# New load order, a TensorE spin and new hand-written orders at both ends of a fused attention and adapter kernel

## The chip, the cores and the metric

The kernel runs on one core of one Trainium2 chip. The metric is the device time of one execution in microseconds (us); three runs of the kernel before gave a median of 393.7 us (393.56 to 393.74). Profiles are of one execution each, and all times inside a profile count from the start of its span.

The engines are named as the profile names them. PE is TensorE's matmul and PEld its weight load, DVE is VectorE, ACT is ScalarE, POOL is GpSimd, SP is SyncE (it only issues DMAs here). "SPq", "ACTq" and "POOLq" are the queues that issue DMAs.

## The reference

Attention over a spatially reduced key grid, and a mixture of eight small adapters on its result. Four batches, 12288 queries of 128 channels each; keys and values are the 4x4 means of a 384x32 grid (768 positions), multiplied by one 128x128 matrix.

```
kv_pool = kv.reshape(B, H//4, 4, W//4, 4, C).mean(axis=(2, 4))
k = v = kv_pool.reshape(B, -1, C) @ w_sr
x = softmax(q @ k.T / sqrt(C)) @ v
logits = x @ w_gate                  # 8 experts, the top two are taken
out = x + sum over the two: weight_e * ((x @ A[e]) @ B[e])
```

## The kernel before, in words

**Tiling.** The 49152 queries are cut into 96 chunks of 512 (24 per batch); four chunks make a group of 2048 queries, loaded together. The 768 keys are six blocks of 128, and are made in three parts h = 0, 1, 2 of two blocks each.

**The stages of a chunk k**, by the names that the order lists use:
- `sc k r` (line 244): scores against the two key blocks of part r. Two 128x512 matmuls into the PSUM tile `sg` (two buffers of two banks), then ACT's exponential into `em`.
- `at k s` (line 254): six matmuls that add the weighted values of 128 queries into the PSUM tile `acc` (one buffer of two banks). The last of its 137 columns carries the sum of weights. `pt k lo hi` (line 423) does the same for key blocks lo to hi of all four quarters.
- `nm k` (line 262): DVE takes the reciprocal and multiplies, which gives `xn`, with the 8 gate logits beside the 128 channels.
- `tp k` (line 281): DVE's eight largest; `ro k` (line 290) and `ga k` (line 308): the weights of the two experts, on POOL with a tanh on ACT.
- `tt x h` (line 317): PE transposes `xn` of chunk x and `hg` of chunk h into one PSUM tile, DVE (V) or ACT (A) copies it out. `dn k` (line 341): down projection into PSUM; `ge k` (line 346): DVE multiplies by the weights, giving `hg`; `up k` (line 355): up projection; `fi k` (line 360): DVE adds `xn` and SP stores 256 KB. The tiles of `tt`, `dn` and `up` share the PSUM tag `mb` with two buffers of one bank.
- Pieces for the ends: `xt`/`cx` (lines 388 and 398) and `hb`/`ht`/`ch` (lines 405 to 413) are the two halves of `tt` apart, `dn2`, `ge2`, `up2` the stages by halves, `af` (line 455) an add and a store, `ca` and `pd` (lines 462 and 467) the same add as a copy on ACT and an add on POOL.

**Order.** Every instruction is recorded in program order on its engine (`tc.keep_in_program_order`, line 65), so the order within an engine is that of the code. Chunks 14 to 71 follow a fixed pattern per chunk (`slot`, line 551). Chunks 0 to 13 and 72 to 95 follow two strings of items written out by hand (lines 579 and 601).

**The first keys.** Batch 0's grid is loaded in fp32 by 24 DMAs of 256 KB (line 98): per part h, four rows r and two halves x. DVE adds row pairs (`ad h i`, line 173), PE transposes with fp32 identity matmuls that also sum the remaining eight pieces (`ky`, line 187), DVE scales (line 206), PE projects (`k2`, line 209; `va`, line 215) and DVE copies out. Later batches are summed on POOL (`pa`, line 162) from 512 KB loads (`kv`, line 96).

**The queries.** Groups 0 and 1 are loaded in fp32 (line 105) and transposed by PE (`tq`, line 107). All later groups are cast to bf16 into DRAM by a DMA that POOL issues (`cq`, line 77, 1 MB read and 512 KB written) and transposed by a DMA that SP issues (`lq`, line 82). The first two casts are issued by `first_casts` (line 506): POOL copies one element of a tile that is being loaded, and so waits for it, then issues both. Before, the element is one of the last load of group 1 (`cs1`).

Of the kernel before, what the change touches and what calls it, by code (L numbers as in the profile page):

```python
# [20 lines left out]
def kernel(  # L21
# [10 lines left out]
    nc = tc.nc  # L32
# [74 lines left out]
    def turn_q(g, m, engine):  # L107
        if g not in qT:
            qT[g] = qpool.tile([P, GT], BF16, tag="qT", name="qT")
        ps = mtile([P, S, P], name="qT_ps")  # L110
        for i in range(S):
            mm(ps[:, i], q_f[g][:, m * S + i], id_f, is_transpose=True,
               start=(i == 0), stop=(i == S - 1))
        o = qT[g][:, m * T:(m + 1) * T].rearrange("p (s t) -> p s t", s=S)
        if engine is nc.scalar:
            keep(nc.scalar.copy(o, ps))
        else:
            keep(nc.vector.tensor_copy(o, ps))
# [6 lines left out]
    load_q(0, 0, GC * S)  # L125
    for h in range(3):
        for r in range(4):
            for x in range(2):
                load_kv(0, h, r, x)
    for m in range(GC):  # L130
        load_q(1, m * S, m * S + S)
    b_f = const.tile([P, C], FP32)
    keep(nc.sync.dma_start(b_f, moe_B.rearrange("e r c -> (e r) c")))
    a_f = const.tile([P, P], FP32)
    keep(nc.sync.dma_start(a_f, moe_A.rearrange("e c r -> c e r")))


    warm = const.tile([P, 1], FP32)
    nc.vector.memset(warm, 0.0)
    keep(nc.scalar.activation(warm, warm, AF.Exp, bias=0.0, scale=1.0))  # L140
    id_f = const.tile([P, P], FP32)
    make_identity(nc, id_f)
    id_bf = const.tile([P, P], BF16)
    nc.vector.tensor_copy(id_bf, id_f)
    wext = const.tile([P, VC], FP32)
    nc.vector.tensor_copy(wext[:, 0:C], w_sr_sb)
    wT_ps = mtile([P, C], name="wT_ps")
    mm(wT_ps, w_sr_sb, id_f, is_transpose=True, start=True, stop=True)
    wT = const.tile([P, C], FP32)
    nc.vector.tensor_copy(wT, wT_ps)  # L150
    w2_ps = mtile([P, E], name="w2_ps")
    mm(w2_ps, wT, w_gate_sb, start=True, stop=True)
    nc.vector.tensor_copy(wext[:, C:VC], w2_ps)


    kfT, vx = {}, {}

    def prepare(b, adder):
# [3 lines left out]
        def pool_step(h, step, lo, hi):  # L162
            t = kvr[b, h]
            if step < 3:
                u, v = t[:, 0].rearrange("p g c -> p (g c)"), t[:, step + 1].rearrange("p g c -> p (g c)")
            else:
                w = 2 * C if step == 3 else C
                u, v = t[:, 0, :, 0:w], t[:, 0, :, w:2 * w]
                keep(adder.tensor_tensor(u, u, v, op=ALU.add))
                return  # L170
            keep(adder.tensor_tensor(u[:, lo:hi], u[:, lo:hi], v[:, lo:hi], op=ALU.add))  # L171

        def pair_step(h, r, x):
            u, v = (kvr[b, h][:, r + i, x] for i in range(2))
            keep(adder.tensor_tensor(u, u, v, op=ALU.add))

        for h in range(3):
            if adder is nc.vector:
                sums.append([lambda h=h, r=r, x=x: pair_step(h, r, x)
                             for r in (0, 2) for x in range(2)])  # L180
                continue
# [5 lines left out]
        def keys(h, half=None):  # L187
            if h == 0 and half != 1:
                st["kpT"] = prep.tile([P, J, P], FP32, tag="kpT", name="kpT")
                kfT[b] = per_b.tile([P, J, P], BF16, tag="kfT", name="kfT")  # L190
            kpT = st["kpT"]
            if half != 1:
                st["ps"] = mtile([P, 2, P], name="kpT_ps")
            ps = st["ps"]
            if adder is nc.vector:
                parts = [(r, i, c) for r in (0, 2) for i in range(2) for c in range(4)]
            else:
                parts = [(0, i, 0) for i in range(2)]
            for n, (r, i, c) in enumerate(parts):
                if half is not None and r // 2 != half:  # L200
                    continue
                mm(ps[:, i], kvr[b, h][:, r, i, c * C:(c + 1) * C], id_f, is_transpose=True,
                   start=(n == 0), stop=(n == len(parts) - 1))
            if half == 0:
                return
            keep(nc.vector.tensor_scalar(kpT[:, 2 * h:2 * h + 2], ps, 1.0 / 16.0, None,
                                         op0=ALU.mult))

        def keys2(h):
            kpT = st["kpT"]  # L210
            ps = mtile([P, 2, P], name="kfT_ps")
            mm(ps, w_sr_sb, kpT[:, 2 * h:2 * h + 2], start=True, stop=True)
            keep(nc.vector.tensor_copy(kfT[b][:, 2 * h:2 * h + 2], ps))  # L213

        def values(h):
# [7 lines left out]
            if adder is not nc.vector:  # L223
                st["vb", h] = prep.tile([P, 2, C], BF16, tag="vb", name="vb")
                keep(nc.vector.tensor_copy(st["vb", h], ps[:, :, 0:C]))
# [8 lines left out]
        for h in range(3):  # L234
            for f in (keys, keys2, values) if adder is nc.vector else (keys, values, turn):
                rest.append(lambda h=h, f=f, **how: f(h, **how))
# [17 lines left out]
    def attend(k, s):  # L254
        b = k // NB
        if k not in acc:
            acc[k] = ps_a.tile([P, S, 256], FP32, tag="acc", name="acc")
        o = acc[k][:, s, 0:VE]
        for j in range(J):
            mm(o, em[k][:, j, s * P:(s + 1) * P], vx[b][:, j], start=(j == 0), stop=(j == J - 1))  # L260
# [11 lines left out]


# [16 lines left out]
    def route(k0):  # L290
        n = size[k0] * S
        eng = nc.gpsimd if k0 > 1 else nc.vector
# [74 lines left out]
    def bank(pool):  # L367
# [20 lines left out]
    def turn_x(k, pool):  # L388
        xT[k] = quad(bank(pool).bitcast(BF16), pool)
        xb = xn[k].bitcast(U16)[:, :, 1::2].bitcast(BF16)  # L390
        for s in range(S):
            mm(xT[k][:, s // 2, s % 2], xb[:, s, 0:C], id_bf, is_transpose=True,
               start=(s % 2 == 0), stop=(s % 2 == 1))

    def copy(engine, o, i):
        keep(nc.scalar.copy(o, i) if engine == "A" else nc.vector.tensor_copy(o, i))  # L396

    def fetch_x(k, engine):
        sb = run.tile([P, S, P], BF16, tag="tt1", name="tt1")
        copy(engine, four(sb), xT[k])  # L400
        xT[k] = sb
# [3 lines left out]
    def hold_h(k, pool):  # L405
        hps[k] = quad(bank(pool).bitcast(BF16), pool)

    def turn_h(k, lo=0, hi=S):
        for s in range(lo, hi):
            mm(hps[k][:, s // 2, s % 2], hg[k][:, s], id_bf, is_transpose=True,  # L410
               start=(s % 2 == 0), stop=(s % 2 == 1))

    def fetch_h(k, lo=0, hi=S, engine="A"):
        if lo == 0:
            hgT[k] = run.tile([P, S, P], BF16, tag="tt1", name="tt1")
        copy(engine, part(four(hgT[k]), lo, hi), part(hps[k], lo, hi))

    def hold_acc(k, pool="sg"):
        acc[k] = bank(pool)
# [3 lines left out]
    def attend_part(k, lo, hi):  # L423
        for s in range(S):
            for j in range(lo, hi):
                mm(acc[k][:, s, 0:VE], em[k][:, j, s * P:(s + 1) * P], vx[k // NB][:, j],
                   start=(j == 0 and s % 2 == 0), stop=(j == J - 1 and s % 2 == 1))

    def down_into(k, pool):
        hp[k] = quad(bank(pool), pool)  # L430
        for s in range(S):
            mm(hp[k][:, s // 2, s % 2], xT[k][:, s], a_bf, start=(s % 2 == 0), stop=(s % 2 == 1))

    def gate_part(k, lo, hi):
        if lo == 0:
# [3 lines left out]
        keep(nc.vector.tensor_tensor(  # L439
            part(four(hg[k]).rearrange("p a b (e r) -> p a (b e) r", e=E), lo, hi),  # L440
            part(four(hp[k]).rearrange("p a b (e r) -> p a (b e) r", e=E), lo, hi),
            part(g4, lo, hi).unsqueeze(3).broadcast_to([P, (hi - lo) // 2, 2 * E, RK]), op=ALU.mult))

    def hold_d(k, pool):
        dp[k] = quad(bank(pool), pool)

    def up_part(k, lo, hi):
        for s in range(lo, hi):
            mm(dp[k][:, s // 2, s % 2], hgT[k][:, s], b_bf, start=(s % 2 == 0), stop=(s % 2 == 1))
# [5 lines left out]
    def add_here(k, lo, hi, queue="SP"):  # L455
        osb = opool.tile([P, S, C], FP32, tag="osb", name="osb")[:, 0:hi - lo]
        keep(nc.vector.tensor_tensor(osb.rearrange("p (a b) c -> p a b c", b=2),
                                     part(four(dp[k]), lo, hi),
                                     part(four(xn[k][:, :, 0:C]), lo, hi), op=ALU.add))
# [57 lines left out]
    def plan(b):  # L517
        if b not in plans:
            plans[b] = prepare(b, nc.gpsimd if b else nc.vector)
# [3 lines left out]
        "tq": lambda g, m, e: turn_q(g, m, nc.scalar if e == "A" else nc.vector),  # L523
        "ad": lambda h, i: plan(0)[0][h][i](),
        "ky": lambda h, half: plan(0)[1][3 * h](half=half),
        "k2": lambda h: plan(0)[1][3 * h + 1](),
        "va": lambda h: plan(0)[1][3 * h + 2](),
        "cs": lambda: first_casts(kvr[0, 2][:, 3, 1, 0:1]),
        "cs1": lambda: first_casts(q_f[1][:, GC * S - 1, 0:1]),
# [10 lines left out]
        "xt": turn_x, "cx": lambda k, e="A": fetch_x(k, e), "hb": hold_h, "ht": turn_h, "ch": fetch_h,  # L540
        "o95": hold_acc, "pt": attend_part, "dn2": down_into, "ge2": gate_part,
# [4 lines left out]
    def follow(order):  # L546
        for item in order.replace("\n", " ").split(";"):
            what, *at = item.split()
# [31 lines left out]
ad 0 0; tq 0 0 A; ad 0 1; ad 0 2; cs1; tq 0 1 A; ad 0 3; ky 0 0; tq 0 2 V; ky 0 1; k2 0; ad 1 0; va  # L580
0; sc 0 0; tq 0 3 A; lq 2; sc 2 0; ad 1 1; ad 1 2; ad 1 3; ky 1 0; sc 1 0; ky 1 1; ad 2 0; sc 3 0;
k2 1; ad 2 1; va 1; sc 3 1; ad 2 2; sc 0 1; ky 2 0; sc 2 1; ad 2 3; kv 1 0 0; ky 2 1; sc 1 1; k2 2;
tq 1 0 V; sc 0 2; va 2; cab; sc 4 2; tq 1 1 V; at 0 2; kv 1 0 1; sc 1 2; at 0 1; sc 4 0; at 0 0; at
# [89 lines left out]
```

## Time and profile before

| what | value |
|---|---|
| median of three runs | 393.7 us |
| the profiled execution | 394.05 us |
| its span | 392.3 us |
| mean granted TensorE clock | 0.994 |
| PE busy from 28 us to 290 us | 261.92 of 262 us |
| em exponential, 128x1024 | 1023 ns, x288 |
| sum of DMA traffic | 76.47 MB, 195 GB/s |

"Busy" adds the time in which an engine has an instruction in work. PE's matmuls are pipelined, so that one matmul's recorded time (379 ns for 512 columns) is longer than the time until the next can end (two of them take 0.43 us in the chain of work); sums of PE work below go by that pitch. The chain of work is followed back from the last instruction to what released each step.

### The profile page before, as it was taken

The numbers are of one execution on the slowest core, as the hardware profiler recorded it, in microseconds if no ns is written. First come the engines' busy times: TensorE is split into PE (matmuls) and PEld (weight loads), VectorE is DVE, ScalarE is ACT, GpSimd is POOL, SyncE is SP. The second block draws the span as 40 slices with busy tenths as digits, with TensorE's granted clock in tenths as the row PEclk, the third lists the DMA queues.
The fourth block names the chain that finished last, engine by engine and source line by source line (L and its number), as shares of the span: only waits on it lengthen the run. The fifth ranks groups of instructions, "written<-read, shape, count | busy, mean of one in ns | idle before, by whom it ended". The sixth has DMA issues, their size and how long they took to land.

```text
span 392.3 us, 11714 instructions
## 1 busy us (share of the span) xinstructions
PE 376.4 (96%) x4589; PEld 302.3 (77%) x4589; DVE 325.3 (83%) x950; ACT 298.0 (76%) x375; POOL 205.0 (52%) x473
## 2 busy tenths in 40 slices
PE   3999999999999999999999999999999899999993
PEld 2767878888887888878888878888786678878882
DVE  2666769989888889888988988989887888888885
ACT  2378988787687787787777877877788787877873
POOL 0010479998331778587432677877524235444443
PEclk9999999999999999999999999999999999999997
DMA  8998969974596989885489999957644566573213
GB/s 296 367 266 222 210 237 245 264 173 136 140 304 145 298 206 342 183 190 135 108 217 256 297 257 295 187 139 134 156 142 110 154 157 148 144 159 105 79 60 136
DMA packets 71464, 76.47 MB, mean 195 GB/s; under 512 B 49936, under 2 KB 50704, under 8 KB 70928
## 3 DMA queue, kind: packets, MB, share of 16 engines
q1 hardware_dynamic: 70272, 63.98, 56.4%
q0 software_dynamic: 704, 11.54, 17.1%
q8 instruction: 36, 0.59, 0.6%
q10 hardware_dynamic: 432, 0.20, 0.2%
q14 instruction: 20, 0.16, 0.1%
HBM read 50.53 MB, written 36.70 MB: 222 GB/s over the span
## 4 chain that ended last, share of the span: by engine, by line
PE 85%; DMA 5%; SPq 3%; DVE 3%; POOL 2%; issue 1%; ACT 1%; ACTq 0%; DVEq 0%; POOLq 0%
PE acc L68 33%; PE sg L68 29%; PE tt_ps L68 10%; PE h_ps L68 5%; PE d_ps L68 5%; SPq L98 3%; DMA qT<-qbf 2%; DMA w_sr_sb<-in_w_sr_dram 1%; DMA kvr<-in_kv_dram 1%; PE v_ps L68 1%; PE kpT_ps L68 1%; DVE tts L335 1%; POOL kvr L171 1%; DVE xn L268 1%; ACT tt L396 0%
## 5 line engine op out<-in xcount | busy, mean ns | idle before, releaser
L252 ACT ACTIVATE em<-sg 128x1024 f16<-128x1024 f32 x288 | 280.9, 1023 | 75.6 <-PE sg L68 74.7
L68 PE MATMUL sg<-qT,kfT 128*128 128x512 bf16 x576 | 170.4, 379 | 0.4 <-DVE kfT L213 0.2
L68 PE MATMUL acc<-vx,em 128*128 128x137 f16 x2280 | 168.1, 223 | 0.0
L68 PEld LDWEIGHTS <-em 128*128 128x128 f16 x2304 | 146.1, 98 | 3.1 <-DVE xn L268 1.1
L68 PEld LDWEIGHTS <-tts 128*128 128x128 bf16 x740 | 56.1, 98 | 43.9 <-issue 2.8
L171 POOL TENSOR_TENSOR kvr<-kvr 128x512 f32<-128x512 f32 x54 | 67.5, 1274 | 13.1 <-DVE tts L335 13.1
L268 DVE TENSOR_TENSOR xn<-acc,rinv 128x544 f32<-128x544 f32 x95 | 68.8, 725 | 3.3
L349 DVE TENSOR_TENSOR hg<-h_ps,gw 128x512 bf16<-128x512 f32 x93 | 64.2, 690 | 7.0 <-PE h_ps L68 0.2
L335 DVE COPY tts<-tt_ps 128x1024 bf16<-128x1024 bf16 (+1 forms) x93 | 61.6, 663 | 2.6 <-PE tt_ps L68 1.6
L362 DVE TENSOR_TENSOR osb<-d_ps,xn 128x512 f32<-128x512 f32 x89 | 61.2, 690 | 0.0
L299 POOL TENSOR_TENSOR over<-xn,srt 128x64 f32<-128x64 f32 (+1 forms) x116 | 30.4, 283 | 56.0 <-DVE srt L286 56.0
L313 POOL TENSOR_TENSOR gw<-th,over 128x64 f32<-128x64 f32 (+1 forms) x58 | 17.0, 294 | 64.0 <-ACT th L311 63.7
L68 PEld LDWEIGHTS <-kfT 128*128 128x128 bf16 x576 | 45.6, 98 | 2.9 <-DVE kfT L213 1.0
L264 DVE RECIPROCAL rinv<-acc 128x4 f32<-128x4 f32 x95 | 17.4, 183 | 35.1 <-PE acc L68 34.5
L68 PEld LDWEIGHTS <-xn 128*128 128x128 bf16 x384 | 28.9, 98 | 20.0 <-DVE xn L268 0.4
L68 PE MATMUL d_ps<-b_bf,tts 128*128 128x128 bf16 x364 | 35.1, 219 | 1.6 <-DVE tts L335 1.1
L68 PE MATMUL h_ps<-a_bf,tts 128*128 128x128 bf16 x372 | 36.0, 219 | 0.3 <-ACT tts L333 0.3
L68 PE MATMUL tt_ps<-id_bf,xn 128*128 128x128 bf16 x372 | 35.8, 219 | 0.0
L68 PE MATMUL tt_ps<-id_bf,hg 128*128 128x128 bf16 x368 | 35.6, 219 | 0.0
L286 DVE MAX8 srt<-xn 128x8 f32<-128x8 f32 x380 | 34.3, 154 | 0.0
L68 PEld LDWEIGHTS <-hg 128*128 128x128 bf16 x384 | 25.8, 98 | 1.7 <-issue 0.4
L305 POOL TENSOR_SCALAR over<-over 128x64 f32<-128x64 f32 (+1 forms) x58 | 19.5, 336 | 5.3
(83 smaller groups left out, 208.5 us busy)
## 6 DMA issues: line engine op xcount, KB each, us to landing
out_dram<-osb SPq DMA_DIRECT2D x94, 256.0 KB, 3.6
kvr<-in_kv_dram SPq DMA_DIRECT2D x36, 512.0 KB, 6.1
qbf<-in_q_dram POOLq DMA_DIRECT2D x22, 512.0 KB, 6.2
kvr<-in_kv_dram SPq DMA_DIRECT2D x24, 256.0 KB, 5.1
qf<-in_q_dram SPq DMA_DIRECT2D x1, 1024.0 KB, 5.1
qf<-in_q_dram SPq DMA_DIRECT2D x4, 256.0 KB, 5.3
out_dram<-osb SPq DMA_DIRECT2D x3, 128.0 KB, 2.3
qT<-qbf SPq DMA_TRANSPOSE x22, 5.5
```

Source lines behind the costliest of these rows:

```text
L68: return keep(nc.tensor.matmul(*a, **k))
L171: keep(adder.tensor_tensor(u[:, lo:hi], u[:, lo:hi], v[:, lo:hi], op=ALU.add))
L252: keep(nc.scalar.activation(em[k][:, 2 * r:2 * r + 2], ps, AF.Exp, bias=0.0, scale=scale))
L264: keep(nc.vector.reciprocal(ri, acc[k][:, :, VC]))
L268: keep(nc.vector.tensor_tensor(x, acc[k][:, :, 0:VC], ri.unsqueeze(2).broadcast_to([P, S, VC]), op=ALU.mult))
L286: keep(nc.vector.max(srt[k0][:, m, s], xn[k][:, s, C:VC]))
L299: keep(eng.tensor_tensor(d, lg, so[:, :, i].unsqueeze(2).broadcast_to([P, n, 8]), op=ALU.subtract))
L305: keep(eng.tensor_scalar(mask, mask, 0.0, None, op0=ALU.is_ge))
L313: keep(eng.tensor_tensor(w[:, 0:n], th, mask, op=ALU.mult))
L335: keep(nc.vector.tensor_copy(sb[:, lo:hi], ps[:, lo:hi]))
L349: keep(nc.vector.tensor_tensor(hg[k].rearrange("p s (e r) -> p (s e) r", e=E), hp[k].rearrange("p s (e r) -> p (s e) r", e=E), gw[k0][:, m ...
L362: keep(nc.vector.tensor_tensor(osb, dp[k], xn[k][:, :, 0:C], op=ALU.add))
```

## The change

1. **Loads.** The SP queue's first loads follow a short list. `lkv h r x` loads row r of part h (both halves at once, 512 KB, where x is "-"), `lf g a b` a piece of query group g (512 KB for two chunks), `lab` the adapter matrices.

```
+lkv 0 3 -; lkv 0 2 -; lkv 0 0 -; lkv 0 1 -; lf 0 0 2; lf 1 1 2; lf 0 2 4; lkv 1 2 -; lkv 1 3 -; lkv
+1 0 -; lkv 1 1 -; lkv 2 3 -; lkv 2 2 -; lkv 2 1 1; lkv 2 0 1; lkv 2 0 0; lkv 2 1 0; lf 1 0 1; lab;
+lf 1 2 4
-    load_q(0, 0, GC * S)
-    for h in range(3):
-        for r in range(4):
-            for x in range(2):
-                load_kv(0, h, r, x)
-    for m in range(GC):
-        load_q(1, m * S, m * S + S)
```

2. **The spin.** Eleven matmuls of 512 columns on a tile of zeros are PE's first instructions.

```
+    idle = const.tile([P, T], BF16)
+    keep(nc.vector.memset(idle, 0.0))
+    def spin(n):
+        ps = mtile([P, T], name="spin_ps")
+        for i in range(n):
+            mm(ps, idle[:, 0:P], idle, start=True, stop=True)
+    spin(11)
```

3. **The first keys** have functions of their own, which take the PSUM tile and the engine from the list. Six row additions stay on DVE instead of twelve; where a pair isn't added, PE transposes both rows, so that PE has 72 fp32 transposes for batch 0 instead of 48. Some of the scaling and copying goes to ACT.

```
+    def turn_k(h, half, x):
...
+        rows = [2 * half] if (h, 2 * half, x) in summed else [2 * half, 2 * half + 1]
...
+        for r in rows:
+            for c in range(4):
+                mm(first_ps[h][:, x], kvr[0, h][:, r, x, c * C:(c + 1) * C], id_f, is_transpose=True,
...
+    def mean_k(h, engine):
+        o = first_kp[0][:, 2 * h:2 * h + 2]
+        if engine == "A":
+            keep(nc.scalar.mul(o, first_ps[h], 1.0 / 16.0))
```

4. **The casts.** The list has `cs k` in place of `cs1`: POOL now watches row 3 of part 2, which the new load order has as the first load of that part.

```
+        "cs": lambda w: first_casts(kvr[0, 2][:, 3, 1, 0:1] if w == "k" else
+                                    q_f[1][:, GC * S - 1, 0:1]),
```

5. **Halves.** A chunk's `acc`, or a tile of the tags `acc` and `sg` that carries another stage, lies in two PSUM banks of two quarters each. `nh k h` normalizes one half; `use` tells the scheduler that instructions on different halves have no dependency. `hd`, `db`, `xb`, `hb` take a tile at one place of the list, and the stage uses it at a later one.

```
+    def use(key, lo, hi, inst):
+        if key not in split:
+            return
+        mine = set(range(lo // 2, (hi + 1) // 2))
+        for other, theirs in users.setdefault(key, []):
+            if not mine & theirs:
+                tc.declare_no_dep(inst.ins, other.ins, reason="other PSUM bank")
+        users[key].append((inst, mine))
```

6. **The lists** for chunks 0 to 13 and 72 to 95 are new; `slot` is as before. All routing is on POOL now (before, DVE routed chunks 0 and 1). The beginnings:

```
-ad 0 0; tq 0 0 A; ad 0 1; ad 0 2; cs1; tq 0 1 A; ad 0 3; ky 0 0; tq 0 2 V; ky 0 1; k2 0; ad 1 0; va
-0; sc 0 0; tq 0 3 A; lq 2; sc 2 0; ad 1 1; ad 1 2; ad 1 3; ky 1 0; sc 1 0; ky 1 1; ad 2 0; sc 3 0;
-k2 1; ad 2 1; va 1; sc 3 1; ad 2 2; sc 0 1; ky 2 0; sc 2 1; ad 2 3; kv 1 0 0; ky 2 1; sc 1 1; k2 2;
-tq 1 0 V; sc 0 2; va 2; cab; sc 4 2; tq 1 1 V; at 0 2; kv 1 0 1; sc 1 2; at 0 1; sc 4 0; at 0 0; at
+init; kb 1 mb; kb 0 sg; ky 0 1 0; cs k; ad 0 1; ky 0 1 1; ky 0 0 0; tq 0 1 A sg; lq 2; ky 0 0 1; kc
+0 A; hd 6 sg; tq 0 0 A mb; hd 5 sg; k2 0 sg V; kb 2 mb; tq 0 2 A acc; kv 1 0 0; tq 0 3 V sg; ad 1 3;
+tq 1 1 A mb; va 0 acc V; sc 0 0; sc 2 0; ky 1 1 0; sc 1 0; ad 1 0; kv 1 0 1; ky 1 1 1; sc 5 0; ky 1
+0 1; ky 1 0 0; pt 0 0 2; kc 1 A; sc 3 0; k2 1 sg A; ad 2 3; ad 2 1; ky 2 1 0; va 1 mb A; kv 1 0 2;
+a2 2 1; kv 1 0 3; sc 0 1; sc 3 1; ky 2 0 0; ky 2 0 1; kc 2 A; sc 1 1; k2 2 mb V; sc 2 1; lq 3; tq 1
+2 V mb; sc 0 2; va 2 mb V; pt 0 2 4; sc 6 2; pt 0 4 6; nm 0; sc 6 0; tq 1 3 V mb; sc 1 2; pt 1 0 2;
```

and the ends:

```
-4; ch 95 2 4; up2 95 0 2; af 93 0 4; ht 94 0 2; ch 94 0 2; up2 95 2 4; af 95 0 2; af 95 2 4; ht 94 2
-4; ch 94 2 4; db 94 mb; up2 94 0 2; af 94 0 2 ACT; up2 94 2 4; af 94 2 4
+tt 92 89 A; db 90 mb; dn2 91 0 4; ro 93; at 94 0; ga 93; hd 95 mb; nm 95; at 94 1; ge2 91 0 4; xt 93
+0 4; at 94 3; tp 95; at 94 2; ht 88 0 2; ht 90 2 4; cx 93 0 2 A; cx 93 2 4 A; ht 90 0 2; ch 88 0 2
+A; dn2 93 0 4; ht 88 2 4; up2 89 0 4; nh 94 0; hb 91 sg; ch 90 0 4 A; ro 95; nh 94 1; hb 92 mb; ga
...
+A; up2 91 0 4; af 93 0 4 SP; ge 94; ch 95 2 4 A; up2 92 2 4; up2 92 0 2; tt - 94 A; af 91 0 4 SP;
+up2 95 0 4; af 92 0 2 ACT; af 92 2 4 ACT; af 95 0 4 SP; up2 94 0 4; af 94 0 4 ACT
```

## The prediction

> **What bounds the kernel now.** I read the page's first two parts, then the busy time by stage, then the two ends. Busy us of 28, 262, 33, 57 and 13 us:
>
> ```profile
> 0.00:28.00 28.00, 20.26 (x116) 15.19 (x117) 14.05 (x31) 12.16 (x15) 2.08 (x9) 1.00 0.98 326
> 28.00:290.00 262.00, 261.92 (x3282) 212.02 (x3280) 227.13 (x680) 207.59 (x251) 161.64 (x310) 1.00 0.83 208
> 290.00:323.00 33.00, 31.10 (x393) 24.23 (x391) 27.10 (x73) 25.93 (x34) 11.68 (x44) 1.00 0.53 138
> 323.00:380.00 57.00, 57.00 (x731) 46.15 (x730) 49.57 (x143) 46.79 (x64) 25.22 (x100) 1.00 0.45 121
> 380.00:393.00 13.00, 6.16 (x82) 4.72 (x78) 7.40 (x26) 5.56 (x14) 4.40 (x10) 0.79 0.29 104
> ```
>
> The first pair is the stage and its length; then PE, PEld, DVE, ACT, POOL, the clock, the DMA engines' share and GB/s. From 28 us PE never waits: a microsecond counts only if it leaves PE's work or one of its gaps. The gaps are the head, 1.9 us in 290:323, and the end. The head's share of 0.98 says that it is bound by DMA: 7.4 MB must come before the third key part is whole. Adding the per-microsecond GB/s of that view gives 5.87 MB by 18 us, 6.65 by 20, 7.06 by 21 and all 8.6 by 26. The rows that end the head (line numbers in front of the operation):
>
> ```profile
> 25.68 0.18 POOL L507 COPY late<-qf 128x1 f32<-128x1 f32 x1 [24.38 <-DMA qf<-in_q_dram]
> 25.80 1.26 POOL L79 DMA_DIRECT2D qbf<-in_q_dram  x2
> ...
> 26.10 0.60 PE L68 MATMUL sg<-qT,kfT 128*128 128x512 bf16 x2
> ```
>
> At 26.10 PE starts sc 0 2, the first scores on part 2. The last query piece is seen by POOL at 25.68, when 8.46 MB have passed at 24.9: a load is usable 0.8 us after its bytes. Then POOL issues both casts, behind all other loads.
>
> **What the casts cost the DMA engines.** Queue 0 carries only them:
>
> ```profile
> q0 software_dynamic: 704, 11.54, 17.1%
> ...
> qbf<-in_q_dram POOLq DMA_DIRECT2D x22, 512.0 KB, 6.2
> ```
> ```profile
> 26.00:27.00 1.00, 0.92 (x7) 0.75 (x7) 0.73 (x2) 0.26 (x1) 1.00 (x2) 1.00 0.00 0
> 27.00:28.00 1.00, 1.00 (x11) 0.79 (x9) 0.71 (x3) 1.00 (x2) 0.07 (x1) 1.00 3.10 524
> ```
> ```profile
> 113.22 0.54 SPq L96 DMA_DIRECT2D kvr<-in_kv_dram  x1
> 116.46 0.33 SPq L363 DMA_DIRECT2D out_dram<-osb  x1
> 116.84 4.76 SPq L96 DMA_DIRECT2D kvr<-in_kv_dram  x1
> ```
>
> 17.1% of 16 engines for 392.3 us, over 22 casts, is 3.05 us of all 16 engines for one cast. The two of the head fill 27.5 to 33.0 us (share 0.95 in 27:33): 5.5 us. They begin 1.8 us after POOL's copy. The SP rows show what another load meets: an issue of 0.54 us takes 4.76 when a cast starts at 116.8, and the rate falls from 559 to 119 GB/s in the next microsecond.
>
> **The change, part by part.**
>
> *Casts (cs k), the largest term.* POOL now watches row 3 of part 2. Ahead of it and with it stand 2.10 MB (part 0), 1.31 (three query pieces), 2.10 (part 1), 0.52, and 0.07 of weights: 6.10 MB, past at 18.6 us, usable at 19.4. The casts then take the engines at 19.4 + 1.8 = 21.2 us, with 7.1 MB past of 8.6. Still out are about 0.5 MB of keys and, last of all, lf 1 2 4. Undisturbed it lands at 25.9 + 0.8 = 26.7 us; behind both casts at 26.7 + 5.5 = 32.2, behind one at 29.8. Its reader is tq 1 2 on PE, directly ahead of sc 0 2; PE's queue behind it is everything, and nothing can pass. I take both casts: the load is issued only when row 2 of part 2 is down (20.6 us at the earliest, its semaphore being reused), when POOL has issued both. sc 0 2 starts after four fp32 transposes (0.44), at 32.7 instead of 26.10: **+6.6**. If the casts yielded to the loads it would be 27.2: +1.1.
>
> [...]
>
> *Keys first.* Part 0 is whole after 2.17 MB instead of 3.2, about 2.5 us sooner, so scores start near 12 us instead of 14.74. By sc 0 2 PE has then done more: one sc more (0.43), eight attention matmuls (0.48), one tq more (0.44): **-1.35**. The scores before it are 9 against 8, so little of the earlier start is kept: ACT needs 1.02 for each, and parts 1 and 2 come no sooner.
>
> *24 more fp32 transposes* (0.105 each by the weight loads, 0.42 for four): 2.5 us of PE, hidden in the wait for part 2; without that cover +2.5. Six DVE sums less (0.69 each): 4.1 us of DVE off a chain whose two last sums stood at 22.23 to 23.66; that is inside the landing-to-score distance above.
>
> *Spin.* 11 matmuls at 0.43 cold: 1.1 to 5.8 us, before w_sr lands (5.3 us after issue, 6.0). Nothing, at most +0.9 if w_sr comes at 4.9. It warms PE: eight fp32 weight loads took 1.57 us at 9.2 and 1.01 at 21.5. But the data sets the pace there: 0 (gain at most 0.6 for each of three such groups, 1.8).
>
> *Clock after the stall.* With PE empty from about 26.4 to 32.2 the clock can fall: it is 0.50 in 388:390, after sparse work.
>
> ```profile
> 386.00:388.00 2.00, 1.15 (x12) 0.80 (x12) 1.68 (x5) 1.06 (x4) 0.75 (x1) 0.90 0.22 82
> 388.00:390.00 2.00, 0.37 (x2) 0.10 (x1) 0.66 (x2) 0.00 (x0) 0.00 (x0) 0.50 1.05 383
> ```
>
> PE was slow at the start from 6.2 to about 11.6 us; half of that, 2.7, is the upper end, 0 the lower. I take **+1.0**, nearer the lower, since ACT shares the limit there (1.02 for each 0.43 of sc). [...]
>
> *Chunks 14 to 71.* PE's sequence is the same instruction by instruction: 216.7 us by the pitches of the chain (sg 0.216, acc 0.060, others 0.056). 0. New waits for a tile's bank and `use`, which only removes waits: 0.
>
> *The end.* The first score of chunk 72 starts at 286.70 before, so the last list takes 105.6 us for 94.2 us of PE work by the same pitches, in both kernels. The new list keeps 4.67 us of PE work behind the last attention matmul (84 small ones) instead of 2.45 (44), so the attention could end at 286.7 + 89.5 = 376.2 instead of 382.2. Behind it DVE has the last normalization (0.6 for the second half) and 8.3 us (12 products and sums by 0.69, of which two by halves) instead of 5.55, then 3.2 us from the last sum to the end of the span, as before (389.12 to 392.3): 388.5 at best, -3.8. Against it: ACT has 99.2 us of instructions by its rows in this list (88.5 before), of which 72 exponentials overlap by 0.10 each (2.86 us for three): 92 of PE's 94.2. Six stores on ACT wait for DVE with exponentials behind them. If ACT's full durations bound, with 4.2 behind them (up, sum, store) and 3 us of waits, it takes 106.4: +0.8, and +3 with DVE late too. Between -3.8 and +3 I take **-2.5**, nearer the row with PE full, as in 323:380.
>
> *The rest* (routing of chunks 0 and 1 on POOL, 0.25 for 0.19 each; smaller SP list): beside full PE, 0.
>
> **Sum:** +6.6 - 1.35 + 1.0 - 2.5 = +3.75 on the profiled execution's 394.05 (span 392.3 and 1.75 around), 397.8. The median lies 0.35 lower: 393.7 + 3.75 = **397.4 us**.
>
> **The rivals.**
> 1. *Forecast, 0.55:* loads behind the casts. With one cast and clock 0 the sum is +4.2 - 1.35 - 2.5 = +0.35, 394.0; with both, 2.7 for the clock and nothing at the end, +7.95, 401.6. Own range 394.0 to 401.6.
> 2. *The loads pass, faster, 0.33.* The engines finish the descriptors they already hold, so lf 1 2 4 lands near 26.7: +1.1 - 1.35 - 2.5 = -2.75, 391.0; with the spin's 1.8 and the best end (-3.8), -5.85, 387.9. For it: at 116 to 117 us the DMA rate stays at 559 while the first cast packets start. Against: the 4.76 us issue. It decides when lf 1 2 4 is down before 29.5 us (26.7 + 2.75).
> 3. *The new end is slower, 0.12.* ACT or its waiting stores bound it, +3 instead of -2.5, on top of the stall: 393.7 + 9.25 = 402.9, and 396 without the stall.
> 4. *The spin on zeros does not warm PE:* inside the cases, since it is priced at 0.
>
> **Range and chances.** 389.0 to 401.5: the lower tenth is the best of case 2, the upper the worst of 1 and 3. A measurement of this kernel tells 0.2% (0.8 us) from no change. Case 1 gives 0.51 slower and 0.04 the same, case 2 0.29 faster, 0.03 the same and 0.01 slower, case 3 0.12 slower: faster 0.29, same 0.07, slower 0.64.
>
> **What would show it.** Right: POOL's copy at about 19.4 us; the DMA rate from queue 0 from 21.2; PE idle in front of the fp32 transposes of qf near 26 to 32 us, released by the load of qf; sc 0 2 near 32.7; chunk 14 some 6 us later than before (70 us); PE full until the last attention matmul, and that about 9 us ahead of DVE's last sum, not 7 (382.2 to 389.12). Wrong: no wait for qf over 1 us (rival 2), PE gaps between chunks 72 and 92 released by ACT (rival 3), or a clock of 1 throughout (the clock term).

## The result: 398.96 us, 1.3% slower, and the profile after

| | before | after |
|---|---|---|
| median us (lowest to highest) | 393.65 (393.56 to 393.74) | 398.96 (397.80 to 399.85) |
| profiled execution, us | 394.05 | 398.47 |
| its span, us | 392.3 | 396.7 |

The ratio is 1.0133, with a 95% interval of 1.0104 to 1.0162. The new kernel's executions lie 2 us apart, those of before 0.2. The profiled one is 4.4 us behind its counterpart, the medians 5.3. (The profiled execution of before is not among the four of the median.)

Busy time by stage after the change; the columns are those of the stages shown for the kernel before: stage, length, PE, PEld, DVE, ACT, POOL, clock, DMA share, GB/s.

```profile
0.00:28.00 28.00, 23.20 (x144) 16.15 (x146) 7.20 (x17) 14.26 (x20) 2.07 (x9) 1.00 0.97 325
28.00:34.00 6.00, 2.33 (x9) 1.94 (x10) 0.69 (x1) 0.41 (x2) 0.00 (x0) 0.59 1.00 203
34.00:290.00 256.00, 253.25 (x3143) 207.26 (x3194) 219.18 (x657) 202.64 (x246) 162.28 (x316) 1.00 0.79 204
290.00:323.00 33.00, 32.63 (x380) 25.13 (x384) 24.62 (x86) 31.88 (x39) 8.56 (x29) 1.00 0.55 122
323.00:380.00 57.00, 55.62 (x724) 45.88 (x734) 44.61 (x157) 51.08 (x76) 36.07 (x109) 1.00 0.42 120
380.00:397.00 17.00, 10.88 (x163) 9.35 (x160) 12.31 (x36) 8.08 (x23) 8.63 (x28) 0.92 0.46 173
```

Before, PE was full from 28 us on. Now the stretch from 28 to 34 us holds 2.33 us of PE work, at a mean clock of 0.59, while the DMA engines are full. (PE's 23.20 us before 28 us include 4.5 of the spin.) The timeline of PE shows where the hole begins and ends:

```profile
26.40 0.59 PE L68 MATMUL sg<-qT,kfT 128*128 128x512 bf16 x2
31.67 1.09 PE L68 MATMUL tail_ps<-id_f,qf 128*128 128x128 f32 x4 [4.67 <-DMA qf<-in_q_dram]
32.55 1.06 PE L68 MATMUL sg<-qT,kfT 128*128 128x512 bf16 x2
```

The second row is tq 1 2: PE stood idle for 4.67 us, until the load of qf, and sc 0 2 starts at 32.55 instead of 26.10. POOL's and SP's own timelines show what was issued ahead of that load:

```profile
19.65 0.18 POOL L601 COPY late<-kvr 128x1 f32<-128x1 f32 x1 [18.36 <-DMA kvr<-in_kv_dram]
19.78 1.26 POOL L79 DMA_DIRECT2D qbf<-in_q_dram  x2
```
```profile
19.62 0.39 SPq L136 DMA_DIRECT2D a_f<-in_moe_A_dram  x1
20.88 2.85 SPq L105 DMA_DIRECT2D qf<-in_q_dram  x1
```

Both casts are issued at 19.78, right after row 3 of key part 2; lf 1 2 4 is issued at 20.88, and the issue takes 2.85 us where a neighbour takes 0.39. In the packet records the casts' 32 packets of 32 KB run from 23.14 to 29.56 us. All 128 packets of 4 KB of lf 1 2 4 start between 28.24 and 31.02.

To see where time is made up I count score pairs by their weight loads: the 43rd begins chunk 14, the 217th opens the last list. Start times in us, and how far the new kernel is behind:

| | before | after | behind by |
|---|---|---|---|
| sc 0 2 (PE) | 26.10 | 32.55 | 6.45 |
| first score of chunk 14 | 67.70 | 74.44 | 6.74 |
| first score of the last list | 286.65 | 292.92 | 6.27 |
| last attention weight load | 381.92 | 384.34 | 2.42 |
| end of the span | 392.27 | 396.69 | 4.42 |

All of the loss is made before chunk 14, and the end list gives 1.85 us back.

### The profile page after: what moved, and what is told of

Its sections match the earlier page's. It is cut to its first block, busy times and chain, and to the rows that moved or that the text cites. A ratio compares the mean times of both kernels' runs of the same rounds, so it can differ in the third digit from the quotient of the medians.

```text
span 396.7 us, 11736 instructions
## 1 busy us (share of the span) xinstructions
PE 377.9 (95%) x4551; PEld 305.7 (77%) x4624; DVE 308.6 (78%) x951; ACT 308.4 (78%) x401; POOL 217.6 (55%) x489
## 4 chain that ended last, share of the span: by engine, by line
PE 77%; DMA 7%; POOL 7%; ACT 3%; issue 3%; DVE 1%; SPq 1%; DVEq 0%; POOLq 0%; ACTq 0%
PE acc L68 31%; PE sg L68 24%; PE tt_ps L68 9%; DMA qf<-in_q_dram 5%; PE h_ps L68 4%; PE d_ps L68 4%; ACT em L319 3%; DMA kvr<-in_kv_dram 2%; PE tail_ps L68 2%; POOL osb L562 2%; POOL over L380 1%; PE v_ps L68 1%; POOL over L385 1%; POOL gw L394 1%; DVE rinv L333 1%
## 5 line engine op out<-in xcount | busy, mean ns | idle before, releaser
L68 PE MATMUL sg<-qT,kfT 128*128 128x512 bf16 x503 | 155.5, 381 | 0.3
L68 PEld LDWEIGHTS <-tts 128*128 128x128 bf16 x676 | 50.5, 98 | 33.4 <-ACT tts L414 0.6
L337 DVE TENSOR_TENSOR xn<-acc,rinv 128x544 f32<-128x544 f32 x88 | 63.7, 724 | 3.0
L416 DVE COPY tts<-tt_ps 128x1024 bf16<-128x1024 bf16 (+1 forms) x83 | 54.3, 658 | 4.6 <-PE tt_ps L68 4.4
L430 DVE TENSOR_TENSOR hg<-h_ps,gw 128x512 bf16<-128x512 f32 x58 | 40.1, 692 | 5.0 <-POOL gw L395 0.5
L443 DVE TENSOR_TENSOR osb<-d_ps,xn 128x512 f32<-128x512 f32 x58 | 40.1, 691 | 0.0
L68 PE MATMUL tt_ps<-id_bf,xn 128*128 128x128 bf16 x344 | 32.9, 219 | 0.9
L68 PE MATMUL tt_ps<-id_bf,hg 128*128 128x128 bf16 x332 | 32.1, 219 | 0.3 <-DVE hg L531 0.3
L68 PE MATMUL h_ps<-a_bf,tts 128*128 128x128 bf16 x284 | 27.3, 219 | 0.9
L68 PE MATMUL d_ps<-b_bf,tts 128*128 128x128 bf16 x252 | 24.4, 219 | 0.8
```

Of the source, the lines that this page charges most:

```text
L68: return keep(nc.tensor.matmul(*a, **k))
L337: keep(nc.vector.tensor_tensor(x, acc[k][:, :, 0:VC], ri.unsqueeze(2).broadcast_to([P, S, VC]), op=ALU.mult))
L416: keep(nc.vector.tensor_copy(sb[:, lo:hi], ps[:, lo:hi]))
L430: keep(nc.vector.tensor_tensor(hg[k].rearrange("p s (e r) -> p (s e) r", e=E), hp[k].rearrange("p s (e r) -> p (s e) r", e=E), gw[k0][:, m ...
L443: keep(nc.vector.tensor_tensor(osb, dp[k], xn[k][:, :, 0:C], op=ALU.add))
```

## The experiments

The theory: the casts, moved ahead of the last query load, hold it back; PE stalls for it and loses its clock. The rivals: the load is late because its issue is late, whatever the casts do; or the loss is made elsewhere (the end list, the spin). All runs stand in one table. A ratio is to the executions of before that were taken with that run, not to the 393.65 of the first row. "sc 0 2", "chunk 14" and "list to end" (from the first score of the last list to the end of the span) are read in each kernel's trace as above.

| run | median us (range) | ratio to before (95%) | sc 0 2 | chunk 14 | list to end |
|---|---|---|---|---|---|
| before | 393.65 (393.56 to 393.74) | 1 | 26.10 | 67.70 | 105.62 |
| after | 398.96 (397.80 to 399.85) | 1.0133 (1.0104 to 1.0162) | 32.55 | 74.44 | 103.77 |
| e1_casts_last | 393.34 (392.87 to 394.42) | 0.9994 (0.9984 to 1.0003) | 27.56 | 69.00 | 103.77 |
| e2_query_ahead | 396.89 (395.67 to 397.06) | 1.0075 (1.0055 to 1.0094) | 30.91 | 72.83 | 103.72 |
| e3_no_spin | 399.19 (398.45 to 399.43) | 1.0125 (1.0097 to 1.0153) | 32.37 | 74.75 | 104.10 |
| e4_old_head_new_end | 392.50 (391.64 to 392.58) | 0.9963 (0.9950 to 0.9976) | 26.16 | 67.76 | 103.74 |
| e5_new_head_old_end | 401.32 (400.62 to 401.83) | 1.0194 (1.0179 to 1.0209) | 32.53 | 75.28 | 105.94 |
| e6_second_cast_last | 394.30 (393.66 to 395.85) | 1.0017 (1.0001 to 1.0033) | 29.33 | 69.58 | 103.79 |
| e7_spin_in_stall | 397.15 (396.71 to 398.19) | 1.0081 (1.0054 to 1.0107) | 32.62 | 72.87 | 103.78 |
| e8_ahead_no_spin | 396.84 (392.34 to 398.78) | 1.0051 (1.0019 to 1.0082) | 31.95 | 74.51 | 104.02 |
| f1_casts_at_last_key | 391.68 (391.39 to 392.49) | 0.9948 (0.9935 to 0.9960) | 26.84 | 67.09 | 104.03 |
| f2_last_key_no_spin | 391.86 (391.11 to 392.71) | 0.9951 (0.9937 to 0.9964) | 27.23 | 67.48 | 104.13 |
| f3_old_head_spin_new_end | 392.29 (392.01 to 392.97) | 0.9962 (0.9950 to 0.9975) | 26.34 | 68.82 | 103.88 |
| f4_query_before_keys | 392.89 (392.34 to 395.66) | 0.9986 (0.9971 to 1.0001) | 28.38 | 68.63 | 103.76 |

### Head and end apart

e4 has the load list, head list and cast trigger of before and no spin; e5 has the end list of before:

```
e4: -lkv 0 3 -; ... ; -ky 0 1 0; cs k; ...   +the load and head lists of the kernel before
e5: -nm 70; sc 72 1; ...                      +the last list of the kernel before
```

> Only the end of the change: load list, head list and cast trigger of the kernel before, no spin; chunks 72 to 95 by the new list. By the two traces the new kernel was 6.27 us behind at the first score of chunk 72 and 4.42 at the end of the span, so the new end list gives 1.85 us: 391.8 us (391 to 392.6). Rival (the new end list is slower, and the head cost less than its trace shows): above 394.5.

> Only the head of the change: new load order, spin, head list and casts of the new kernel; chunks 72 to 95 by the list of before. If the terms add, this is the stall and its clock with nothing given back: 393.65 + 6.3 = 400 us (399 to 401.5), with sc 0 2 near 32.5 us. Rival (the loss is made in the end list): 393 to 395.

392.50 and 401.32: the end list alone wins, the head alone loses 1.9%, so the rival that puts the loss into the end list (B) falls. The two differences, -1.15 and +7.67 us, add up to 6.5, not to the 5.3 of both together. In the profiled execution of e5 PE's clock came back at 37.66 us, in that of the new kernel at 35.90, and that alone was worth 0.86 us (see the clock term below). From the first score of the last list to the end of the span all kernels with the new list take 103.7 to 104.1 us, those with the old one 105.6 and 105.9: the end does not depend on the head.

### Whose fault is the late load?

e1 puts the trigger of the casts back to the last query piece; e2 leaves it and issues the load three places earlier; e6 delays the second cast alone.

```
e1: -ky 0 1 0; cs k;                        +ky 0 1 0; cs q;
e2: -lkv 2 1 0; lf 1 0 1; lab; lf 1 2 4     +lkv 2 1 0; lf 1 2 4; lf 1 0 1; lab
e6:      keep(nc.gpsimd.tensor_copy(late, watch))
    -    for g in range(2, 4):
    -        cast_q(g)
    +    cast_q(2)
    +    keep(nc.gpsimd.tensor_copy(late, q_f[1][:, GC * S - 1, 0:1]))
    +    cast_q(3)
```

> The changed kernel, but POOL issues the two head casts when the last query piece (lf 1 2 4) has landed, as the kernel before did, instead of row 3 of key part 2. Theory (the casts stand ahead of lf 1 2 4 on the DMA engines): that load lands near 26.7 us, sc 0 2 starts at 27.0 to 27.5 us instead of 32.55, the clock stays at 1.0 between 29 and 36 us, and of the 6.65 us that chunk 14 lost 5.1 to 5.5 come back for the stall and 1 to 2 for the clock: 391.5 to 393 us. Rival A (the load is late because its issue waits at 20.88 us for a free semaphore, whatever the casts do): sc 0 2 stays past 31 us and the time near 399. Rival B (the loss is made in the end list): under 1 us is won, 398 to 399.

In e1 SP issues lf 1 2 4 even later than in the new kernel, at 21.42 us, but the issue takes 0.34 us and PE never waits for the load. So the rival that blames the late issue (A) falls. Nor is the length of the issue the cause: in e5, which has the same head as the new kernel, it took 0.33 us (from 21.49), and PE waited 4.59 us all the same. SP's and PE's timelines of e1:

```profile
21.42 0.34 SPq L105 DMA_DIRECT2D qf<-in_q_dram  x1
32.71 3.20 SPq L84 DMA_TRANSPOSE qT<-qbf  x1
```
```profile
27.12 0.60 PE L68 MATMUL tail_ps<-id_f,qf 128*128 128x128 f32 x4
27.56 0.59 PE L68 MATMUL sg<-qT,kfT 128*128 128x512 bf16 x2
...
38.02 0.60 PE L68 MATMUL sg<-qT,kfT 128*128 128x512 bf16 x2 [1.01 <-DMA qT<-qbf]
```

The stall and the half clock are gone, and yet the time is 393.34, 0.3 us above what was expected. The last row tells most of it: the casts now end at 34.81 us, and sc 8 0, which the new list has early, waits 1.01 us for the transposed queries that they feed. Late casts have a price as well, paid 10 us later.

> The changed kernel, but only the first of the two head casts is issued at row 3 of key part 2; the second waits for lf 1 2 4. Theory: lf 1 2 4 stands behind one cast instead of two. A cast is 2.4 to 2.75 us of all engines, so sc 0 2 starts at 29.6 to 30.3 us instead of 32.55, and the clock keeps 1.0 or falls for one stretch of 3.4 us: 394.5 to 397 us. If the wait had nothing to do with the casts: 398 to 400.

One cast ahead gives one half: sc 0 2 at 29.33, 3.2 us earlier than with two, PE's wait 2.16 us, and no loss of clock. 394.30, a little under the range expected.

> The changed kernel, but lf 1 2 4 is issued three places earlier, ahead of lf 1 0 1 and of the adapter loads; the casts keep their trigger. Theory: the load's bytes are in the queues before the casts' packets start at 23.4 us, so it lands before 26 us although the casts run as early as before; PE goes through to sc 0 2 without a wait of more than 0.5 us (27.0 to 27.6 us), the clock stays at 1.0, and the time is 391.5 to 393. If the casts delay every load whose bytes are not yet moved, wherever it stands in the issue order, tq 1 2 still waits past 30 us and the time stays above 396. The loads that now follow the casts (lf 1 0 1, the adapters) land near 31 us; their readers come after 34 us, so they should cost nothing.

This one went against me. PE still waits, 3.49 us:

```profile
26.36 0.59 PE L68 MATMUL sg<-qT,kfT 128*128 128x512 bf16 x2
30.45 0.65 PE L68 MATMUL tail_ps<-id_f,qf 128*128 128x128 f32 x4 [3.49 <-DMA qf<-in_q_dram]
```

The packet records tell why. Of the 4 KB packets of lf 1 2 4 all but three start by 24.81 us. The other three start at 26.87, 27.05 and 29.61. The records don't name the engine, but these are the times at which cast packets end: the first sixteen, of 2.43 us each, end between 26.65 and 27.48, the second sixteen between 29.09 and 30.07. PE starts on the load at 30.45, after its last packet, so 3 of 128 cost nearly as much as all. To be issued ahead of the casts wasn't enough here. The rule that I took from it, to be tested in f1: the bytes are to be through before the casts' packets start.

### The rule put to use

```
f1: e2's load list, and
 "cs": lambda w: first_casts(kvr[0, 2][:, 3, 1, 0:1] if w == "k" else
+                            kvr[0, 2][:, 1, 0, 0:1] if w == "l" else
-ky 0 1 0; cs k;   +ky 0 1 0; cs l;
f4: -lkv 2 3 -; ... lab; lf 1 2 4   +lf 1 2 4; lkv 2 3 -; ... lab
```

> The changed kernel with lf 1 2 4 ahead of lf 1 0 1 and the adapters, and with the two head casts issued when the last key piece (lkv 2 1 0) has landed, near 23.5 us, instead of row 3 of key part 2 (near 20 us) or the last query piece (27.0 us). Theory (a load loses to the casts only with the bytes that have not moved when their packets start): the packets start at 25.2 us or later, lf 1 2 4 has moved by 24.9, PE does not wait for it (sc 0 2 at 27.2 to 27.6), and the transposes for qT 2 come 1.5 to 3 us earlier than with the casts last, so that sc 8 0 no longer waits 1.0 us for them. Chunk 14 0.1 to 0.3 us behind the kernel before, time 392.0 to 392.6. Rival (any cast before the last query piece has landed delays it): PE waits 2 us or more for tq 1 2, time above 394.5.

391.68 us, better than both kernels and a little under the range expected: POOL's copy stands at 23.60, the last packet of lf 1 2 4 ends at 24.55, and the casts' packets start at 25.19. PE in f1 goes through, and is full from 28 to 323 us:

```profile
26.41 0.60 PE L68 MATMUL tail_ps<-id_f,qf 128*128 128x128 f32 x4
26.84 0.59 PE L68 MATMUL sg<-qT,kfT 128*128 128x512 bf16 x2
```
```profile
28.00:34.00 6.00, 6.00 (x66) 4.60 (x64) 3.65 (x12) 5.38 (x7) 0.99 (x4) 1.00 0.90 182
34.00:290.00 256.00, 256.00 (x3218) 207.21 (x3216) 221.33 (x661) 203.41 (x247) 162.51 (x318) 1.00 0.78 209
290.00:323.00 33.00, 33.00 (x387) 25.08 (x384) 23.59 (x84) 31.94 (x41) 9.68 (x31) 1.00 0.58 121
```

> The changed kernel with lf 1 2 4 issued ahead of all of key part 2; the casts keep their trigger, row 3 of key part 2, which now lands 1.25 us later. It asks whether the query load is special or whatever stands last in line. Theory (whatever is last): tq 1 2 never waits, but the last key pieces (lkv 2 0 0, lkv 2 1 0) end near 24.6 us, just as the casts' packets start, and their stragglers stand behind casts on some engines: PE waits for kvr before the transposes of part 2 instead of for qf, 2 to 5 us, 394.5 to 399 us. If only the query load was in danger: no wait over 0.5 us for either, 391.8 to 393.

The time is the one given for the other case, 391.8 to 393. The wait did move to the keys, but it is 0.99 and 0.19 us, not 2 to 5, and PE runs on at a clock of 1.0. The longer wait ends at 22.16 us, before the first packet of the casts (24.39), so the casts didn't make it: 512 KB more stand ahead of these keys. Whether keys that are still out would be held back as the query load was is therefore not shown. Nine of the ten executions lie at 392.3 to 393.2; the tenth took 395.66. Whether that one had the longer stall can't be told, since it was not profiled. PE in f4:

```profile
22.16 1.09 PE L68 MATMUL tail_ps<-id_f,kvr 128*128 128x128 f32 x8 [0.99 <-DMA kvr<-in_kv_dram]
...
24.77 1.72 PE L68 MATMUL tail_ps<-id_f,kvr 128*128 128x128 f32 x12 [0.19 <-DMA kvr<-in_kv_dram]
```

### What the clock costs

```
e7: -lq 3; tq 1 2 V mb; sc 0 2;   +lq 3; wm 20; tq 1 2 V mb; sc 0 2;
```

> The changed kernel with 20 more matmuls on zeros directly ahead of tq 1 2, in the 4.67 us in which PE waits for its load. Theory: the stall stays (sc 0 2 at 32.0 to 32.6 us), but the clock stays at 1.0, and the PE work between 31.7 and 36.15 us, which ran at 0.5, runs at full speed: 1 to 2 us come back, and the runs scatter less. If the lower clock costs nothing there (ACT is the limit of those scores): within 0.4 us of the changed kernel.

It separates the stall from its after-effect. PE, clock, DMA share and GB/s of 28 to 36 us, first e7, then the changed kernel:

```profile
28.00:32.00 4.00, 3.81 (x18) 1.00 0.63 175
32.00:36.00 4.00, 3.79 (x35) 1.00 1.04 267
```
```profile
28.00:32.00 4.00, 0.33 (x2) 0.63 1.03 214
32.00:36.00 4.00, 4.00 (x21) 0.51 0.99 285
```

From 32 to 36 us e7 gets through 35 matmuls, the changed kernel through 21. sc 0 2 is at 32.62 in e7, as late as ever; chunk 14 starts 1.57 us earlier. That is the price of the half clock. That the runs would scatter less is not borne out: 1.5 us between them against 2.05.

### The spin

```
e3 (from the changed kernel), e8 (from e2), f2 (from f1): -    spin(11)
f3 (from e4): +    spin(11)
```

> The changed kernel without the 11 matmuls on zeros. Theory (the head waits for data, so a warm PE in it is worth nothing): the clock turns to 1.0 some 5 to 7 us later than at 5.4 us, the transposes of part 0 run at half speed, but tq 1 2 still waits for its load to 31.5 us and sc 0 2 starts at 32.4 to 32.8; time within 1 us of the changed kernel. Rival (the spin is worth what it was put in for): sc 0 2 starts 1 us later or more, and the time is 1 to 2 us longer.

> The changed kernel with lf 1 2 4 issued ahead of lf 1 0 1 and of the adapters, and without the spin at the start. It tells what the spin is worth when no later wait hides it. Theory (the data sets the pace of the head): within 0.5 us of the same kernel with the spin. Rival: 1 to 2 us slower than it, since the cold transposes push the scores on parts 0 and 1 back and nothing absorbs that any more.

> The same without the 11 matmuls on zeros: the price of the spin where no stall follows that could hide it. Theory (data sets the pace of the head): within 0.4 us of the same kernel with the spin. Rival (a cold PE is late with the 24 more transposes): sc 0 2 starts 0.5 us or more later and the time is longer by as much.

> Load list, head list and casts of before, the new end list, and the spin of 11 matmuls on zeros at the start. Against the same kernel without spin (392.5 us): 0 to 0.4 us faster if the head is bound by its data, 1 us or more faster if the cold clock up to about 11 us is what holds it; slower by more than 0.4 if the spin delays the first transposes.

e3 against the changed kernel is 399.19 to 398.96, f2 against f1 391.86 to 391.68, f3 against e4 392.29 to 392.50: no difference outside the executions' own spread. (f3's chunk 14 is 1.06 us later than e4's in the profiled executions, which the medians do not show: the one profiled of f3 took 392.97 us, its longest.) The trace shows that the spin does warm PE (the clock turns to 1.0 at 4.43 us in f1, at 9.61 in f2), and where the gain stops. The same 24 transposes of part 0, first in f1, then in f2:

```profile
7.26 3.10 PE L68 MATMUL sg<-id_f,kvr 128*128 128x128 f32 x24 [0.66 <-DMA kvr<-in_kv_dram]
10.95 0.66 PE L68 MATMUL sg<-id_f,qf 128*128 128x128 f32 x4 [0.60 <-DMA qf<-in_q_dram]
```
```profile
6.51 4.33 PE L68 MATMUL sg<-id_f,kvr 128*128 128x128 f32 x24 [0.46 <-DMA kvr<-in_kv_dram]
11.30 0.66 PE L68 MATMUL sg<-id_f,qf 128*128 128x128 f32 x4 [0.46 <-DMA qf<-in_q_dram]
```

1.2 us faster, but in both the next group waits for qf; 0.39 us is left at chunk 14 (67.09 against 67.48).

e8 decides nothing on the spin: its ten executions run from 392.34 to 398.78 us, and the one profiled is the slowest. That fits a load whose last packets sometimes slip through ahead of the casts, but only that one execution was profiled (the load's last packet starts at 30.44, PE waits 3.69 us). The ratio of e8 in the table is that of eight of the ten, without the two longest.

## Why the prediction was right, and which terms were off

The direction and the mechanism held: 398.96 lies in the range of 389.0 to 401.5 and in the forecast's own of 394.0 to 401.6. The sum was made for the profiled execution, where it gave +3.75; +4.42 was measured. That it came so near is in part luck: the sum had the clock and the end list each some 0.65 us too good, and chunks 14 to 71 gave 0.47 back. Term by term:

| step | predicted | measured | from |
|---|---|---|---|
| stall at tq 1 2 (sc 0 2 later) | +6.6 | +6.45 | 32.55 against 26.10 |
| work done ahead | -1.35 | -1.35 | f1: sc 0 2 +0.74, chunk 14 -0.61; e6: +3.23, +1.88 |
| clock | +1.0 | +1.64 | 6.74 - 6.45 + 1.35; e7 gives 1.57 |
| chunks 14 to 71 | 0 | -0.47 | 6.27 - 6.74 |
| end list | -2.5 | -1.85 | 4.42 - 6.27 |
| sum | +3.75 | +4.42 | |

- *Casts.* POOL's copy was priced at 19.4 us and came at 19.65; both casts stand ahead of the load and cost two, as taken (one: e6). The step in between failed. I let the casts start 1.8 us after the copy, at 21.2; they start 3.5 us after it, at 23.14, with SP's loads still running (384 GB/s from 21.14 to 23.14). The end comes out nearly the same, 31.7 against 32.2, since none of the packets of lf 1 2 4 started in those 2 us. The long SP issue (4.76 us) that the prediction held against rival 2 was no sign of this: the stall came with an issue of 2.85 us and, in e5, with one of 0.33. That the engines finish what they already hold, as rival 2 supposed, no run shows: in e2 the load was issued at 17.71 us, the casts at 20.32, and three of its packets started after the first casts' packets had ended at 26.65; in the new kernel the adapter loads, issued at 18.42 and 19.62, landed 10.9 and 10.6 us later.
- *The start of the casts.* With all engines at work on SP's loads the first cast packet came 3.2 us (e5) to 4.1 us (e6) after POOL's copy, 3.5 in the new kernel, and 1.6 us in e1, f1 and the kernel before, where the loads had all but run out. Between the two rounds of cast packets a part of the load passed in e5: ten of its 128 packets start from 25.85 to 27.64 us, the other 118 from 28.43 on. In the new kernel none slipped in. What kept the first cast packet back is not shown here.
- *Keys first* was right to 0.01 us, and the 24 more transposes and the spin were hidden as said. With the stall gone (f1) sc 0 2 is 0.74 us behind the kernel before, well under the 2.5 priced for no cover.
- *Clock*: mis-sized, 1.0 for 1.6. I leaned on ACT sharing the limit; it didn't here: from 32 to 36 us, with PE at half speed, ACT is busy for 1.02 us and waits for PE. The trace of the new kernel has the clock's changes at 5.18, 29.08, 35.90 and 394.30 us. The distances of 23.89, 6.83 and 358.40 us are 7, 2 and 105 times 3.413 us; in the kernel before, 375.47 us (12.12 to 387.59) are 110 times that. So the stall is read here in stretches of 3.41 us, counted from the fall at 29.08; columns are PE, clock, DMA share, GB/s:

```profile
25.67:29.08 3.41, 1.28 (x5) 1.00 0.80 192
29.08:32.49 3.41, 0.82 (x4) 0.50 1.18 227
32.49:35.90 3.41, 3.41 (x18) 0.50 0.94 279
```

The stretch ahead of the fall still held 1.28 us of PE work, 38%; after the next, with 0.82, the clock stayed at 0.50; after the first full one it was 1.0 again. In e2, with an idle time of 3.49 us, one stretch at half speed followed (30.92 to 34.33). In e5 the stretch from 30.83 to 34.24 held 2.59 us of work, 76%, and still another one at half speed followed, up to 37.66. In e6, with 2.16 us idle, the stretch from 24.77 to 28.18 was 55% busy and the clock stayed. The busy share alone doesn't tell these cases apart: in the kernel before the clock fell at the end, behind a stretch that was 63% busy with small matmuls (384.17 to 387.58). Nor does the stall's length alone fix the price; that it goes with where the stall falls among the stretches is my estimate from e2 (one at half speed), e5 and the new kernel (two each), and no run moved the stall alone. By the sum of the table's clock row it was 1.67 us in e2, 2.13 in e3 and 2.50 in e5, whose stall was no longer than the new kernel's.

- *Chunks 14 to 71* were priced at nothing. They take 218.95 us in the kernel before, 218.96 in e7, and 218.47 to 218.50 in the other twelve, with either head and either end. The half microsecond sits at single places (before: 0.28 of it between the 121st and the 127th score pair; e7: 0.47 between the 61st and the 67th). Whether it belongs to the code or to the one execution profiled was not tried; the profiled execution of before lies 0.40 us above the median of its kernel, that of e7 0.26, which would fit the latter.
- *End list*: right in sign, mis-sized. PE, PEld, DVE, ACT, POOL, clock, DMA share and GB/s of the last list up to the last attention and behind it, before and after:

```profile
286.70:382.10 95.40, 93.50 (x1197) 75.07 (x1195) 81.30 (x229) 76.85 (x104) 38.91 (x153) 1.00 0.48 127
382.10:392.30 10.20, 4.06 (x46) 2.62 (x43) 5.72 (x20) 4.02 (x11) 3.42 (x6) 0.77 0.36 131
```
```profile
292.90:384.60 91.70, 90.00 (x1142) 73.19 (x1157) 70.86 (x250) 82.15 (x116) 47.86 (x147) 1.00 0.47 121
384.60:396.70 12.10, 6.28 (x85) 4.75 (x82) 7.84 (x19) 6.11 (x18) 4.61 (x16) 0.90 0.50 189
```

The attention ends 91.4 us into the list, not 89.5 by the best case, and 12.35 us are left behind it instead of 10.35. So 3.86 us are won and 2.0 given back. Rival 3 (ACT or its stores make the new end slower) is out: 103.7 to 104.1 us in every kernel that has the list, against 105.6 before, and the waits of PE in it that the profile names (0.7 us) are for DVE. The given-back part is a chain at the very end, POOL's gates, DVE, PE, ACT, PE, DVE, for one chunk with nothing beside it:

```profile
389.97 0.69 DVE L531 TENSOR_TENSOR hg<-sg,gw 128x512 bf16<-128x512 f32 x1 [0.47 <-POOL gw L395]
...
390.72 0.40 PE L68 MATMUL tt_ps<-id_bf,hg 128*128 128x128 bf16 x4 [0.26 <-DVE hg L531]
...
391.15 0.59 ACT L414 COPY tts<-tt_ps 128x512 bf16<-128x512 bf16 x1 [0.59 <-PE tt_ps L68]
...
391.80 0.40 PE L68 MATMUL sg<-b_bf,tts 128*128 128x128 bf16 x4 [0.46 <-ACT tts L414]
391.84 1.28 DVE L551 TENSOR_TENSOR osb<-sg,xn 128x512 f32<-128x512 f32 x2
```

- *The medians* differ by 5.3 us, the profiled executions by 4.4, because the profiled execution of before lies 0.40 us above its median and that of the new kernel 0.49 below. What makes the new kernel's executions scatter stays open. The clock's price, 1.6 us in one execution and 2.5 in another for the same stall, can be a part of it; but e7, whose clock never fell in its profile, scatters nearly as much.

## What to carry to other kernels

A transfer that was issued early, because its own reader is far away, was paid for here by the load that stood behind it: 4.67 us of idle PE behind two casts, 2.16 behind one (e6). PE started on that load behind its last packet (in e2 that one starts at 29.61 us, PE at 30.45). So time the big, patient transfer by when the last urgent byte has moved, neither by the order of issue nor by the last urgent landing: in f1 the load ended at 24.55, the casts' packets started at 25.19, and PE did not wait. A stall on PE like these, of 3.49 us (e2) to 5.12 (e3), is to be priced with the clock on top, here 1.6 to 2.5 us. And where one change moves two ends of a kernel, measure the ends apart: here one half was worth -0.4% and the other +1.9%, and the sum hid both.

## What the runs showed of the hardware

- The two casts (DRAM to DRAM) move in 32 packets of 32 KB, in two rounds of 16, of 2.43 us each in the new kernel and up to 3.9 us in f3. Three 4 KB packets that came behind such packets held back a load whose other packets were through 2 to 5 us before (e2).
- SP's issue of the load took 2.85 us in the new kernel, 2.78 in e6, 0.34 in e1 and 0.33 in e5. In e5 the load was as late as in the new kernel, so the length of an issue doesn't tell when its load lands.
- The casts' first packet came 1.6 us after POOL's copy where the other loads had all but run out (before, e1, f1), 3.2 to 4.1 us after it where they had not (new kernel, e2, e5, e6).
- The changes of PE's clock lay whole multiples of 3.413 us apart: 7, 2 and 105 in the new kernel, 110 in the kernel before. It fell behind a stretch of 3.41 us that was 38% busy (new kernel), so that one was not empty. It stayed through one of 55% (e6) and fell behind one of 63% at the end of the kernel before, so the busy share alone did not decide. After the fall in the stall another stretch at half speed followed one of 76% (e5), and a clock of 1.0 followed a full one (new kernel, at 35.90 us; e2, at 34.33).
